# A new issue order for the steady part of a fused short convolution, RMS norm and SwiGLU layer

## The chip, the cores and the metric

The kernel runs on one core of a Trainium2 chip, as one program. The metric is the device time of one execution in microseconds. Shown times are medians of runs on the same chip; the profile is of one further execution, with its own time.

## What is computed

The first stage is a lightweight convolution: softmax weights of 7 taps for each of 8 heads, applied causally along 4096 positions to 8 sequences of 192 channels. The result, 32768 tokens of 192 channels, goes through an RMS norm and a SwiGLU layer of 1536 hidden units, all in float32.

```python
w = softmax(weight, axis=-1)                          # 8 heads x 7 taps
out = np.einsum('hk,bskhg->bshg', w, x_unf)           # causal, 7 taps
x = out.reshape(B * S, D)                             # 32768 x 192
xn = x / sqrt(mean(x * x, -1) + 1e-06) * rms_g
g, val = xn @ w_gate, xn @ w_val                      # 192 x 1536 each
return (g / (1 + exp(-g)) * val) @ w_out              # 1536 x 192
```

## The kernel before, in words

The 32768 tokens are cut into 32 pairs of two tiles of 512 tokens. Pairs 0 and 1 are worked out plainly while the weights are prepared. From pair 2 on, each pair is one block of the steady part: 68 products (gate and value side by side, line 948) and 42 output steps (line 976) on TensorE. Both matrix products are done as 2 x 2 block products with seven instead of eight multiplications, so that sums of blocks stand around them: sums of the input (words x and n, l, d, where n, l and d also split each operand into three parts of fewer bits), sums of products (f1, f3, f4, f5, f6), sums of the hidden values (h1 to h4) and sums of outputs (c1, s7, c2, C22, C21). The hidden units come as six columns of 256, numbered 0 to 5. Columns 0, 2, 4 and 5 take eleven products each, P1 to P7 and Q1 to Q4; columns 1 and 3 take twelve each, A, B and E of the four cells a, b, c and d of the block product.

The order of everything in a block is written out by hand, as words:

- LINE (line 131) is the order of TensorE's 110 words. `P5.2` is product P5 of column 2; `o4.1` is output form 4 with column 1. Before, words 0 to 67 are products, 68 to 109 steps.
- ORDER (line 81) is one round, used for pairs 3 to 31 and once more to finish the last: `p3` issues the next three words of LINE; `Vma.1` issues the word ma.1 on VectorE. The first letter is the engine: V is VectorE, A ScalarE, G GpSimd, S the DMA queue of SyncE. A `+` or `-` at the end means the next or the previous pair, `++` the pair after the next.
- SECOND (line 98) is the round of pair 2, FIRST (line 115) that of pair 1. What FIRST has done ahead for a later pair is not done again in the second round.

`run` (at the end) reads the words. An engine takes its words strictly in this order, and waits for what a word needs from other engines, so a word that has to wait holds up those behind it on its engine. The words that matter here:

- ga to gd are the gates: ScalarE reads a product bank and writes silu into `tt` (line 1031). ma to md multiply by the other half of the bank on VectorE (line 1038) and so make the hidden values. Only when both are done is the bank free; there are four banks, taken and given back by `open` and `give`.
- f1 copies a bank (ScalarE, line 705), f3 copies the first product into c to `tt`. f4 and f5 add on VectorE (line 1025). In column 5 the fifth sum is written to `tt` and f6 adds it to d (line 1018). P7 may add into bank b only after f4 has read it, and Q3 and P4 only after f5.
- h1 to h4 (line 1003) run on VectorE (V) or GpSimd (G); o7 needs h3, o6 needs h2, o3 needs h4 and o5 needs h1. o1 must have read a column before h2 overwrites it, o2 before h4 does.
- C22 and C21 (line 1055) add up the outputs and T11, T12, T21, T22 (line 991) transpose them into `o_sb`, two instructions each; C22 must be done before the o3 steps add into its bank. The stores are the words st, issued by `leave` (line 1087). For the last pair `leave` is called right after the transposes of each half, on ScalarE's and SyncE's queues in turn.
- cv0 to cv6 are the taps of a later pair (line 474; cv0 on ScalarE, line 470), then sq, red, pow, bc and mul (line 524) its norm. pl puts it away to DRAM (line 1098), ft fetches it back as `xb` (line 676), ld loads x (line 174).
- A piece of weights (line 822) is loaded into one of 12 slots, the ring, when the last product that read the slot has been issued. The 48 pieces of a pair are loaded in the order in which LINE first needs them.

Of the kernel before, what the change touches and what calls it, by code (L numbers as in the profile page):

```python
# [20 lines left out]
def kernel(  # L21
# [58 lines left out]
    )  # L80
    ORDER = (
# [15 lines left out]
    )  # L97
    SECOND = (
# [15 lines left out]
    )  # L114
    FIRST = (
# [14 lines left out]
    )  # L130
    LINE = (
# [7 lines left out]
    )  # L139

    cst = ctx.enter_context(tc.tile_pool(name="cst", bufs=1))
# [1213 lines left out]
```

## Time and profile before

| | |
|---|---|
| median of 3 runs | 2448.26 us (2447.83 to 2448.28) |
| the profiled execution | 2448.45 us, its span 2446.6 us |
| mean granted TensorE clock | 0.999 |
| TensorE, VectorE, ScalarE, GpSimd busy | 99%, 88%, 42%, 17% of the span |
| pieces of the longest chain | products (line 948) 57%, output steps (line 976) 36% |
| start of the first block's products | 208.41 us |

A row of the timeline has the start and the length in microseconds, the engine, the line, the operation, output and inputs, the count, and in brackets the idle time of the engine ahead of it with what ended it. PE is TensorE's matmul, PEld its weight load, DVE VectorE, ACT ScalarE, POOL GpSimd; a q behind the name (SPq, ACTq) is the part of an engine that issues DMAs. A row of the groups has the busy time, the mean in nanoseconds of one, and the idle time ahead. In the wait view a row says which engine waited for which, the total in microseconds, how often, and the longest. In the table of stretches each engine has its busy time and its count, then come the clock, the DMA share and GB/s.

### The profile page before, as it was taken

Reading aid. Unit: us, or ns where it says so; the run is one execution under the profiler, and the core shown is the slowest. Engines: PE = TensorE matmul, PEld = TensorE weight load, DVE = VectorE, ACT = ScalarE, POOL = GpSimd, SP = SyncE. Lnnn points to the kernel's source line nnn. Section 1 sums busy time; section 2 is a strip of 40 time slices with the busy share of each in tenths; the row PEclk is TensorE's granted clock in tenths of the full one; section 3 lists DMA queues with packets and bytes.
Section 4 is the critical chain, followed back from the end, with each engine's and each line's share of the span. In section 5 each row is a group of like instructions: output and inputs, shape, how many; then the busy total and the mean of one; then the engine's idle time right before and its main releaser. Section 6 shows DMA issues by size and latency. Waiting matters only on the chain.

```text
span 2446.6 us, 69165 instructions
## 1 busy us (share of the span) xinstructions
PE 2433.7 (99%) x29136; PEld 1947.4 (80%) x29136; DVE 2164.7 (88%) x2822; ACT 1027.1 (42%) x1431; POOL 412.4 (17%) x362
## 2 busy tenths in 40 slices
PE   8999999999999999999999999999999999999999
PEld 5648888888888878878877888777788777878777
DVE  8688988899888899888899888998888998888975
ACT  6443344443344444344443444433444443444432
POOL 0542011110111110111100111101111101111010
PEclk9999999999999999999999999999999999999999
DMA  7375668666677666677666676666776676776653
GB/s 153 61 212 142 171 179 215 188 166 171 175 189 215 174 170 176 177 200 206 160 175 174 181 212 193 164 170 175 190 213 176 169 176 174 203 207 158 174 161 96
DMA packets 716391, 430.54 MB, mean 176 GB/s; under 512 B 510330, under 2 KB 702386, under 8 KB 716082
## 3 DMA queue, kind: packets, MB, share of 16 engines
q1 hardware_dynamic: 712336, 425.21, 66.5%
q8 instruction: 230, 3.77, 0.7%
q10 hardware_dynamic: 3746, 0.92, 0.2%
q14 instruction: 79, 0.65, 0.1%
HBM read 366.96 MB, written 58.98 MB: 174 GB/s over the span
## 4 chain that ended last, share of the span: by engine, by line
PE 96%; DMA 1%; POOL 1%; DVE 1%; SPq 1%; issue 0%; ACT 0%; DVEq 0%; POOLq 0%
PE ps L948 57%; PE ps L976 36%; PE ps L1135 2%; DMA ht<-in_moe_w_val_dram 0%; PE ps L920 0%; POOL ht L1003 0%; SPq L174 0%; POOL part L799 0%; DMA x<-in_x_dram 0%; DMA wd<-part 0%; DVE ht L1003 0%; DMA ht<-in_moe_w_gate_dram 0%; SPq L258 0%; DVE part L795 0%; DVE ht L1038 0%
## 5 line engine op out<-in xcount | busy, mean ns | idle before, releaser
L948 PE MATMUL ps<-part,ring 64*128 64x512 f32 x11304 | 1327.9, 388 | 0.0
L948 PEld LDWEIGHTS ps<-part,ring 64*128 64x128 f32 x11304 | 1117.9, 184 | 176.7 <-DVE tt L1018 11.3
L1031 ACT ACTIVATE tt<-ps 128x512 f32<-128x512 f32 x744 | 438.6, 599 | 718.4 <-PE ps L948 533.6
L1038 DVE TENSOR_TENSOR ht<-ps,tt 128x512 f32<-128x512 f32 x744 | 494.2, 685 | 149.8 <-ACT tt L1031 145.2
L976 PE MATMUL ps<-ht,wo_sb 128*32 128x384 f32 (+2 forms) x7272 | 443.9, 380 | 0.0
L976 PE MATMUL ps<-ht,x 128*32 128x256 f32 (+2 forms) x6696 | 405.2, 379 | 0.3 <-POOL ht L1003 0.3
L976 PEld LDWEIGHTS ps<-ht,wo_sb 128*32 128x32 f32 x7272 | 311.6, 110 | 103.1 <-issue 11.6
L976 PEld LDWEIGHTS ps<-ht,x 128*32 128x32 f32 x6696 | 287.5, 110 | 95.5 <-POOL ht L1003 0.5
L474 DVE SCALAR_TENSOR_TENSOR y<-xh,tp,y 128x1536 f32<-128x1536 f32 x186 | 338.0, 1817 | 1.2
L1025 DVE TENSOR_TENSOR ps<-ps,tt 128x1024 f32<-128x1024 f32 x210 | 258.5, 1231 | 38.9 <-ACT tt L705 28.4
L503 POOL TENSOR_SCALAR r<-r 128x8 f32<-128x8 f32 x31 | 6.1, 198 | 1598.1 <-DVE r L498 1597.9
L705 ACT COPY tt<-ps 128x384 f32<-128x384 f32 (+1 forms) x182 | 151.9, 834 | 258.1 <-PE ps L976 249.4
L1003 DVE TENSOR_TENSOR ht<-ht 128x512 f32<-128x512 f32 x312 | 213.5, 701 | 10.4 <-PE ps L976 9.2
L705 ACT COPY ps<-ps 128x1024 f32<-128x1024 f32 (+1 forms) x151 | 134.0, 887 | 187.5 <-PE ps L976 91.3
L1003 POOL TENSOR_TENSOR hs<-ht 128x512 f32<-128x512 f32 x90 | 115.3, 1296 | 275.1 <-DVE ht L1038 227.8
L705 ACT CAST part<-tt 128x1024 fp32r<-128x1024 f32 x60 | 62.7, 1045 | 187.4 <-DVE tt L868 187.4
L976 PE MATMUL ps<-hs,x 128*32 128x128 f32 (+2 forms) x2232 | 131.6, 379 | 0.0
L976 PEld LDWEIGHTS ps<-hs,x 128*32 128x32 f32 x2232 | 98.2, 110 | 26.9
L1003 DVE TENSOR_TENSOR ht<-hs,ht 128x512 f32<-128x512 f32 x181 | 117.3, 689 | 0.1
L854 DVE TENSOR_TENSOR part<-xb,part 128x1024 fp32r<-128x1024 f32 x87 | 105.9, 1217 | 0.0
L856 DVE SCALAR_TENSOR_TENSOR part<-part,xb 128x1024 fp32r<-128x1024 f32 x87 | 105.8, 1216 | 0.0
L948 PE MATMUL ps<-part,part 64*128 64x512 f32 x720 | 103.9, 387 | 0.0
(137 smaller groups left out, 1573.0 us busy)
## 6 DMA issues: line engine op xcount, KB each, us to landing
ring<-wd SPq DMA_DIRECT2D x1326, 192.0 KB
xb<-xd SPq DMA_DIRECT2D x60, 512.0 KB
xd<-xh SPq DMA_DIRECT2D x240, 96.0 KB
part<-wd SPq DMA_DIRECT2D x114, 192.0 KB
xh<-in_x_dram SPq DMA_DIRECT2D x192, 105.0 KB
xb<-xd SPq DMA_DIRECT2D x60, 256.0 KB
out_dram<-o_sb SPq DMA_DIRECT2D x126, 96.0 KB
out_dram<-o_sb SPq DMA_DIRECT2D x62, 128.0 KB
```

The lines of the kernel that those rows point to most:

```text
L474: nc.vector.scalar_tensor_tensor(out=y, in0=xk, scalar=w, in1=y, op0=ALU.mult, op1=ALU.add)
L503: nc.gpsimd.tensor_scalar(out=r, in0=r, scalar1=s / D, scalar2=s * 1e-6, op0=ALU.mult, op1=ALU.add)
L705: nc.scalar.copy(out=dst, in_=src)
L854: e.tensor_tensor(out=split_of(g, 1).bitcast(F32R), in0=src, in1=high, op=ALU.subtract)
L856: nc.vector.scalar_tensor_tensor(out=split_of(g, 2).bitcast(F32R), in0=high, scalar=1.0 + SPLIT, in1=src, op0=ALU.mult, op1=ALU.subtract,)
L948: nc.tensor.matmul(out=self.both(j, c)[:, h, :], lhsT=left[HALF[h]], rhs=right[HALF[h]], start=(first and q == 0), stop=True, skip_group_c ...
L976: nc.tensor.matmul(out=self.acc(b)[i * Q : (i + 1) * Q, at : at + n], lhsT=left, rhs=cols, start=fresh, stop=True, skip_group_check=True, ...
L1003: engine[eng].tensor_tensor(out=dst, in0=a, in1=b, op=op)
L1025: nc.vector.tensor_tensor(out=self.both(j, c), in0=self.both(j, "b"), in1=s5, op=ALU.add)
L1031: nc.scalar.activation(out=tt[:, t, :], in_=self.both(j, c)[:, 0, :], func=AF.Silu)
L1038: nc.vector.tensor_tensor(out=self.hv(j, "abcd".index(c)), in0=self.both(j, c)[:, 1, :], in1=tt[:, t, :], op=ALU.mult,)
L1135: nc.tensor.matmul(out=bank(h, bks[h])[:], lhsT=wf[HALF[h], AT[h][k], u * NF + f, :], rhs=xb[HALF[h], g, k, :], start=(k == 0), stop=(k == ...
```

## The change

ORDER, SECOND and LINE are written anew, and three words are added at the end of FIRST. No word's work changes, and each block has the same 68 products and 42 steps. What differs:

- LINE has another order. The three products of column 3's cell c (Ac.3, Bc.3, Ec.3), which stood among column 0's products, now stand among column 5's, right ahead of P7.5. P7.5 moves from word 63 to word 62, Q3.5 from 66 to 67, P4.5 from 67 to 66. The output steps follow another order of columns, and so do all words of ORDER around them.
- Four sums go from VectorE to GpSimd: h3.1, h1.2, h3.3 and h2.1. GpSimd has nine of 24 then, not five.
- The last three words of a pair's LINE (o3.0, o3.2, o3.5) are issued at the start of the next round (`p3-`), and T12, T21 and T22 follow there in this order. Before, T22 and T21 stood at the end of the round, and T12 at the start of the next.
- The tap cv4 goes to the round before (`Vcv4++`). For pair 3 it stands at the end of FIRST, with d.4 of pair 2 (and l.2, which FIRST has done already), ahead of C22 of pair 1 on VectorE. In SECOND d.4 stood behind C22 and T11.
- The loads of x (`Sld`) start earlier in the block, at word 61, not 76, and the stores stand elsewhere.

The diff, cut to the rows that the text speaks of:

```diff
     ORDER = (
-        "p1 Vcv5+ p1 VT12- p1 Af1.0 p2 Vcv4+ p2 Aga.1 Vcv6+ p1 Vma.1 p1 Aga.0 p1 Agb.1 Vma.0",
...
-        "Af1.2 Vcv2+ p2 Agc.1 Vmc.1 Af3.2 p2 Sst0.1- p1 Aga.2 p1 Vf4.2 p2 Asq+ p1 Vma.2 Vf5.2",
...
-        "p1 Vf4.5 p2 Vf5.5 Aga.5 Vma.5 p1 Gh1.4 p2 Sft.4+ Vf6.5 Vh3.2 Agd.5 Gh1.3 p1 Agb.5",
-        "Vh3.3 p1 Vh2.0 p5 Vmd.5 Vmb.5 Ac1 Sft.5+ Vh1.5 Agc.5 p1 An.0+ Sst0.4- p1 Vh3.5",
...
-        "Vd.3+ Ac2 Vh4.3 An.2+ Vl.2+ p2 Vh4.0 p1 Vh4.4 p4 Vd.2+ VC22 p2 VT11 p2 Vx3+ VC21",
-        "An.4+ p2 Acv0++ VT22 VT21 p1 Vd.4+ p1",
+        "p3- p1 Vcv5+ Af1.0 p1 VT12- p1 VT21- p1 Vcv1+ VT22- Aga.1 p1 Vma.1 Vl.4 p1 Aga.0 p1",
...
+        "Agd.1 p2 Vmd.1 Agd.0 p2 Agb.0 p1 Vcv6+ Vmb.0 Sst0.3- Vmd.0 p1 Vcv3+ Af1.2 p1 Sst1.0-",
+        "p1 Agc.1 Vmc.1 p1 Sst0.4- Af3.2 Vf4.2 p3 Sst0.0- p1 Aga.2 Sst1.1- p1 Vma.2 Vf5.2 p1",
...
+        "p2 Sft.0+ Af3.5 Sft.2+ p1 Sft.4+ Gh1.2 p2 Vf4.5 Sld.4++ p2 Sft.5+ Aga.5 Vma.5",
+        "Sld.3++ p1 Agc.3 p1 Vf5.5 Gh3.3 Gh1.4 Vh3.2 p1 Sld.7++ Vmc.3 p2 Vf6.5 Agc.5 p2 Agb.5",
+        "Agd.5 Sld.6++ p1 Vmb.5 p1 Vmd.5 Vmc.5 p1 Vh1.5 Sld.5++ p1 Gh3.4 Vh2.0 Sst1.2- p3 Ac1",
+        "p1 Vh2.3 An.0+ Vh3.5 p2 Vh2.2 Gh2.1 p1 Vx3+ Sld.0++ Vh2.4 p2 Vd.0+ An.1+ p1 Vl.1+",
...
+        "Vd.3+ Acv0++ p1 VC22 Vd.4+ Vcv4++ p5 VC21",
     )
     SECOND = (
-        "p2 Vl.2 VC22- VT11- p6- Vd.4 VT22- VT21- Vcv5+ VT12- p1 Af1.0 p4 Aga.1 Sst0.4-",
+        "p2 VC22- VT11- p6- VT22- VT21- Vcv5+ VT12- Af1.0 p2 Aga.1 p1 Vma.1 Vl.4 p1 Aga.0 p1",
...
     FIRST = (
...
-        "VC21 p1 Vh4.4",
+        "VC21 p1 Vh4.4 Vl.2+ Vd.4+ Vcv4++",
     )
     LINE = (
-        "P1.0 Aa.1 Ba.1 Ea.1 Ab.1 P2.0 Q1.0 Eb.1 Bb.1 P5.0 P6.0 Ad.1 Bd.1 Ed.1 Ac.3 P7.0 P3.0",
-        "Q2.0 Ec.3 Bc.3 Q3.0 Q4.0 P4.0 P1.2 Ac.1 Ec.1 Bc.1 P5.2 P6.2 P2.2 Q1.2 Ab.3 P7.2 P3.2",
-        "Q2.2 Bb.3 Q4.2 Q3.2 P4.2 Eb.3 P1.4 Aa.3 Ea.3 Ba.3 P5.4 P6.4 P2.4 Q1.4 Ad.3 P7.4 Q2.4",
-        "P3.4 Ed.3 Bd.3 Q4.4 P1.5 Q3.4 P4.4 P5.5 P6.5 Q1.5 P2.5 Q4.5 P7.5 P3.5 Q2.5 Q3.5 P4.5",
...
+        "P1.0 Aa.1 Ea.1 Ba.1 P2.0 Q1.0 P5.0 P6.0 Ab.1 Eb.1 Bb.1 Ad.1 P3.0 P7.0 Q2.0 Ed.1 Bd.1",
+        "Q3.0 Q4.0 P4.0 P1.2 Ac.1 Bc.1 Ec.1 P5.2 P6.2 Q1.2 P2.2 Ab.3 P7.2 Eb.3 Q2.2 P3.2 Q4.2",
+        "Q3.2 P4.2 Bb.3 P1.4 Aa.3 Ba.3 Ea.3 P5.4 P6.4 Q1.4 P2.4 Ad.3 Bd.3 P7.4 Ed.3 P3.4 Q2.4",
+        "Q4.4 P1.5 P4.4 Q3.4 P5.5 P6.5 Q1.5 P2.5 Ac.3 Bc.3 Ec.3 P7.5 Q4.5 Q2.5 P3.5 P4.5 Q3.5",
```

50 rows, old and new, of tables (LINE, ORDER, SECOND) are left out of this document.

## The prediction

> **What bounds the kernel now.** I read the page first: its span, the busy shares and the chain that ended last.
>
> ```profile
> span 2446.6 us, 69165 instructions
> ...
> PE 2433.7 (99%) x29136; PEld 1947.4 (80%) x29136; DVE 2164.7 (88%) x2822; ACT 1027.1 (42%) x1431; POOL 412.4 (17%) x362
> ...
> PE 96%; DMA 1%; POOL 1%; DVE 1%; SPq 1%; issue 0%; ACT 0%; DVEq 0%; POOLq 0%
> ```
>
> TensorE bounds. Then the table of stretches, for one block (a pair's 68 products and 42 output steps), with the count and busy time of PE, PEld, DVE, ACT and POOL:
>
> ```profile
> 1252.67:1326.96 74.29, 74.29 (x916) 58.64 (x914) 67.34 (x87) 31.23 (x42) 11.39 (x10) 1.00 0.70 183
> ```
>
> A block takes 74.29 us, at full clock, and thirty of them are nearly the whole span. "Busy" can hide a late start, so the block has to be compared with its own undisturbed pace. The next rows, of the timeline, are PE and its weight loads (PEld) at the start and at the end of this block's products, then the last four products of the block two later; last the wait view from 290 to 2400 us (28 blocks):
>
> ```profile
> 1252.67 1.65 PE L948 MATMUL ps<-part,ring 64*128 64x512 f32 x12
> ...
> 1254.62 3.36 PEld L948 LDWEIGHTS ps<-part,ring 64*128 64x128 f32 x30
> ```
>
> ```profile
> 1298.70 0.86 PE L948 MATMUL ps<-part,part 64*128 64x512 f32 x6
> 1299.49 0.52 PE L976 MATMUL ps<-ht,wo_sb 128*32 128x384 f32 x4
> ```
>
> ```profile
> 1444.98 3.16 PE L948 MATMUL ps<-part,ring 64*128 64x512 f32 x24
> 1448.07 1.29 PE L976 MATMUL ps<-ht,wo_sb 128*32 128x384 f32 x18
> ```
>
> ```profile
> PEld ps L948 <- DVE tt L1018: 10.5, 28, 0.4
> PEld ps L976 <- issue: 10.1, 28, 0.4
> PEld ps L948 <- issue: 5.6, 28, 0.2
> ```
>
> Thirty loads are five products (six matmuls each, two at a time): (3.36 - 0.18 for the last load) / 14 = 0.227 us a pair of matmuls, 0.680 a product. 68 products would take 46.25; the part lasts 1299.49 - 1252.67 = 46.82. Of the 0.57 over, 0.13 is the first product's start (1.65 against 5 x 0.227 + 0.386) and 0.11 the change to output steps (the last pair starts at 1298.70 + 0.45, the step 0.34 later, not 0.227): both stay. That leaves 0.33. Most of it is one place: the last four products take 1448.07 - 1444.98 = 3.09 where 2.72 is the pace, 0.37, less the 0.11 of the change: 0.26 us. The wait view names the cause, the only data wait of TensorE in the steady part: the sum of line 1018 (word f5.5), read before Q3.5 may add into the same bank. No row there names a DMA.
>
> **The change part by part.** I number the words of LINE from 0; product k starts near 0.13 + 0.680 k in its block, and steps follow at 27.43 / 42 = 0.653 us.
>
> (1) f5.5 goes earlier against its reader. These are it and f6.5 now:
>
> ```profile
> 1296.62 1.23 DVE L1018 TENSOR_TENSOR tt<-ps,tt 128x1024 f32<-128x1024 f32 x1 [1.12 <-PE ps L948]
> ...
> 1298.36 1.22 DVE L1018 TENSOR_TENSOR ps<-ps,tt 128x1024 f32<-128x1024 f32 x1
> ```
>
> It waits for P7.5 and ends at 1297.85, 45.18 in the block; Q3.5, word 66, was due at 0.13 + 44.88 = 45.01. P7.5 moves from word 63 to 62 while the first reader (P4.5) stays at 66: f5.5 ends 0.68 earlier, at 44.50, 0.5 ahead. So the 0.26 goes. Also P7.4 and P7.5 each stand further behind the products on which their sum f4 waits (six and seven words, five now), which may take some of the other 0.07. At P7.2 the distance is still five words. I take 0.26 a block, 30 x 0.26 = **-7.8 us**; ends: 0 if another wait takes its place, 30 x 0.33 = -9.9.
>
> (2) Four sums of h move from VectorE to GpSimd.
>
> ```profile
> L1003 DVE TENSOR_TENSOR ht<-ht 128x512 f32<-128x512 f32 x312 | 213.5, 701 | 10.4 <-PE ps L976 9.2
> L1003 POOL TENSOR_TENSOR hs<-ht 128x512 f32<-128x512 f32 x90 | 115.3, 1296 | 275.1 <-DVE ht L1038 227.8
> ```
>
> VectorE loses 4 x 0.70 = 2.8 of its 67.3 us a block, GpSimd gains 4 x 1.30 = 5.2 on 11.4; neither is the bound, so I count nothing. What must not get late is C22, on VectorE, which o3.4 (word 104) awaits. Now:
>
> ```profile
> 1301.30 1.28 DVE L1038 TENSOR_TENSOR ht<-ps,tt 128x512 f32<-128x512 f32 x2
> ...
> 1322.18 0.55 DVE L1055 TENSOR_TENSOR tt<-ps,tt 128x384 f32<-128x384 f32 x1
> ```
>
> C22 ends at 1322.73, o3.4 starts at 1299.49 + 36 x 0.653 = 1323.00: 0.27 to spare, and the 42 steps show no stall. Between f6.5 and C22 the new queue has three h less, and x3 and T11 more (0.60 from start to start each: 1.28 - 0.68; T11 0.56): 1.20 - 0.56 = 0.64 less; some 0.4 of it is spent waiting for the gate of word 67, and the steps come 0.26 sooner. The spare time stays near 0.25.
>
> (3) P5.2 goes from word 27 to 24 and opens the bank that md.0 frees; ahead of md.0 stand md.1, the tap cv6 and mb.0. The nearest rows:
>
> ```profile
> 1268.73 1.09 ACT L1031 ACTIVATE tt<-ps 128x512 f32<-128x512 f32 x2 [1.43 <-PE ps L948]
> ...
> 1270.57 1.81 DVE L474 SCALAR_TENSOR_TENSOR y<-xh,tp,y 128x1536 f32<-128x1536 f32 x1
> 1272.30 0.69 DVE L1038 TENSOR_TENSOR ht<-ps,tt 128x512 f32<-128x512 f32 x1
> 1273.14 1.23 DVE L1025 TENSOR_TENSOR ps<-ps,tt 128x1024 f32<-128x1024 f32 x1 [0.15 <-ACT tt L705]
> ```
>
> A gate starts 0.97 after its last product (1268.73 is 16.06; word 22 starts at 15.09). Word 16 ends d.1: gate at 11.01 + 0.97 = 11.98, done 12.58; then 0.60 for md.1, 1.73 for the tap, 0.60 for mb.0, 0.69 for md.0: 16.2. P5.2 is due at 16.45: 0.2 to spare. f4.2 has as much now (ends 21.70, P7.2 due 21.89), and its place has at most the 0.07 of small delays. So I take 0; the upper end is the stall of f5.5, 0.26 a block.
>
> (4) Transfers. Shortest lead of a ring load (from the end of the last product that read its slot to the first that needs it): by LINE eight products now, 5.4 us, then ten, 6.8 us. So the wait view should still name no DMA. SP's queue gets the loads of x earlier, beside the puts:
>
> ```profile
> L822 SPq DMA_DIRECT2D ring<-wd x1326: 315/320/2059, 199.1 to 2403.4; - x190
> L1098 SPq DMA_DIRECT2D xd<-xh x240: 533/617/2278, 140.4 to 2336.5; - x120
> L676 SPq DMA_DIRECT2D xb<-xd x120: 319/414/1382, 105.6 to 2347.6; - x120
> L174 SPq DMA_DIRECT2D xh<-in_x_dram x255: 464/842/3610, 21.6 to 2283.3; - x128
> ```
>
> By the medians (middle figures, ns), words 42 to 67 issue 20 ring loads (6.4), eight puts (4.9), four fetches (1.7), three loads of x (2.5) and two stores of about 0.5: 16.5 us in 17.7. It fits, without room: 0 taken, price under the rivals.
>
> (5) The head, once: d.4 and one tap stood behind the second pair's C22 and T11 (SECOND), and now stand in FIRST, ahead of C22.
>
> ```profile
> 208.53 0.69 DVE L1003 TENSOR_TENSOR ht<-ht 128x512 f32<-128x512 f32 x1 [0.67 <-PE ps L976]
> 209.13 0.55 DVE L1055 TENSOR_TENSOR tt<-ps,tt 128x384 f32<-128x384 f32 x1
> ...
> 209.99 3.84 PEld L976 LDWEIGHTS ps<-ht,wo_sb 128*32 128x32 f32 x72 [0.36 <-DVE tt L1055]
> ...
> 210.16 1.18 DVE L856 SCALAR_TENSOR_TENSOR part<-part,tt 128x1024 fp32r<-128x1024 f32 x1
> ...
> 212.34 1.77 DVE L474 SCALAR_TENSOR_TENSOR y<-xh,tp,y 128x1536 f32<-128x1536 f32 x1
> ```
>
> C22 ends at 209.68 and TensorE goes on at 209.99; all it has meanwhile are two products of the next pair, which it has done by 209.8. With the two operations ahead, C22 and all behind it come 1.18 + 1.77 less some 0.05 of overlap each: **+2.85 us**. Ends: 0 if something hid it (the h sum ahead waits for TensorE, so nothing does), 2.95.
>
> (6) The tail, once: T22 and T21 now follow T12, which waits for the last step.
>
> ```profile
> 2437.94 1.15 DVE L991 STREAM_TRANSPOSE o_sb<-tt 128x256 f32<-128x256 f32 x4
> 2438.92 2.11 ACTq L1087 DMA_DIRECT2D out_dram<-o_sb  x3
> ...
> 2441.36 0.65 DVE L991 STREAM_TRANSPOSE o_sb<-ps 128x256 f32<-128x256 f32 x2 [2.28 <-PE ps L976]
> 2441.84 2.16 ACTq L1087 DMA_DIRECT2D out_dram<-o_sb  x3
> ```
>
> The 1.15 us of transposes and the first half's stores fall behind the end of TensorE. ScalarE's queue then issues six stores in a row, its last three 2.1 us later than now: **+2.1 us**; ends 1.15 (the transposes alone) and 3.
>
> Sum, against the profiled execution's 2448.45 us (span 2446.6 and 1.85 around it): -7.8 + 2.85 + 2.1 = -2.85, **2445.6**. The median of the runs, 2448.26, lies 0.2 lower: I say **2445.4 us**, -0.12%. A measurement of this kernel can tell about 0.2%, 4.9 us, from no change.
>
> [...] Early on GpSimd and VectorE slow each other, both with two operands in SBUF (first the usual time of the VectorE operation, then the timeline):
>
> ```profile
> L854 DVE TENSOR_TENSOR part<-xb,part 128x1024 fp32r<-128x1024 f32 x87 | 105.9, 1217 | 0.0
> ```
>
> ```profile
> 185.34 9.88 POOL L1003 TENSOR_TENSOR ht<-hs,ht 128x512 f32<-128x512 f32 x5 [7.54 <-PE ps L976]
> ...
> 188.37 2.30 DVE L854 TENSOR_TENSOR part<-ring,part 128x1024 fp32r<-128x1024 f32 x1
> ...
> 1295.19 1.29 POOL L1003 TENSOR_TENSOR hs<-ht 128x512 f32<-128x512 f32 x1
> ```
>
> There a GpSimd sum takes 1.98 (9.88 / 5), not 1.29, and VectorE's 1.22 becomes 2.30. In the steady part GpSimd's sums run beside gates read from PSUM, at full speed (1295.19 beside f5.5). [...]
>
> **The rivals.**
> (A) As summed: 2445.4.
> (B) Faster: all 0.33 a block goes and the tail costs only the transposes: -9.9 + 2.85 + 1.15 = -5.9, **2442.4**. For it: the longer distances of P7.4 and P7.5. Against: P7.2 keeps its five.
> [...]
> (D) Another bank wait takes the place of the old one, at P5.2 or P7.2, at the old price: 30 x 0.26 = 7.8 back, **2453**, at the edge of what can be told. The 0.2 to spare speaks against it, its thinness for it.
> (E) SP's queue: it blocks on the first put until the scaling on GpSimd is done, runs over its 17.7 us, and ring loads come late; 0.5 us a block would be +15, **2460**. Against: the lead grows by 1.4 us.
> (F) The change isn't what its words say: in LINE all three products of column 3 (Ac.3, Bc.3, Ec.3) stand ahead of P7.5, none behind. The sums above use LINE as it stands, so this changes no number.
>
> **How the numbers follow.** A 0.38 (0.03 of it below the 0.2% line), B 0.25 (0.01 above it), D 0.14 (half past the line on the slow side), C 0.13, E 0.10. Faster 0.27 (0.03 + 0.24), within 0.2% 0.43 (0.35 + 0.01 + 0.07), slower 0.30 (0.07 + 0.13 + 0.10). The range runs from 2440.5 (B with the tail near nothing) to 2456, which holds A, B, D and a C of lighter price, and leaves out E and the rest: 0.2. A's own is 2443 to 2448.
>
> **What would show it.** Right: the wait of PEld for line 1018 gone or tiny; blocks of 74.0 us; the first steps after C22 near 212.8 instead of 209.99; after the last step, transposes of 1.8 us and six stores in a row. Wrong: a new row of PE or PEld behind line 1038 (D), 1055 or 1025, steps slower than 0.653 (C), or a row that names a DMA (E); GpSimd's sums above 1.3 us.

## The result, and the profile after

| | before | after the change |
|---|---|---|
| median of 20 runs each | 2448.27 us (2447.72 to 2450.64) | 2453.15 us (2447.44 to 2460.67) |
| the profiled execution | 2448.45 us, span 2446.6 | 2452.15 us, span 2450.4 |
| start of the first block's products | 208.41 us | 208.49 us |
| block of pair 2, of pair 3 | 78.53, 74.29 us | 84.52, 76.11 us |
| blocks of pairs 4 to 30, mean | 74.29 us | 74.06 us (21 of the 27 take 73.92 to 74.03) |
| from the start of the last block to the end | 79.7 us | 81.6 us |

The ratio is 1.0017 (95% interval 1.0010 to 1.0024): slower by 0.17%, where 0.12% faster was forecast. The runs of the changed kernel also spread over 13 us, those of before over 3.

The page's first rows, and then the table of stretches for the blocks of pairs 2, 3 and 9 (columns as in the prediction):

```profile
span 2450.4 us, 69381 instructions
...
PE 2429.1 (99%) x29136; PEld 1979.6 (81%) x29136; DVE 2090.1 (85%) x2702; ACT 1033.3 (42%) x1431; POOL 565.3 (23%) x482
```

```profile
208.49:293.01 84.52, 78.35 (x986) 65.17 (x984) 66.40 (x87) 31.50 (x42) 16.48 (x14) 1.00 0.65 161
293.01:369.12 76.11, 76.00 (x912) 67.15 (x912) 65.44 (x83) 31.52 (x42) 16.48 (x14) 0.98 0.76 179
735.30:809.30 74.00, 74.00 (x918) 63.94 (x914) 64.80 (x83) 31.41 (x43) 16.48 (x14) 1.00 0.76 184
```

The ordinary block is 0.3 us shorter, as forecast. Pair 2's block lasts 84.52 us with PE busy for 78.35 only, and pair 3's has a granted clock of 0.98. The wait view of PEld, 290 to 2400 us:

```profile
PEld ps L976 <- issue: 11.8, 32, 0.7
PEld ps L948 <- issue: 5.9, 29, 0.4
PEld ps L948 <- DVE tt L1055: 4.1, 2, 3.9
PEld ps L948 <- DVE ps L1025: 1.3, 4, 0.4
PEld ps L948 <- DVE ht L1038: 0.3, 1, 0.3
```

The old row (line 1018, 28 times) is gone. In its place stands one long wait, 3.9 us behind line 1055, C21. The timeline of the end of pair 2's block tells what C21 waited for:

```profile
289.06 1.57 ACT L470 ACTIVATE y<-xh,tp 128x1536 f32<-128x1536 f32 x1 [4.73 <-DMA xh<-in_x_dram]
290.67 1.82 DVE L474 SCALAR_TENSOR_TENSOR y<-xh,tp,y 128x1536 f32<-128x1536 f32 x1 [4.69 <-ACT y L470]
292.41 0.55 DVE L1055 TENSOR_TENSOR tt<-ps,tt 128x384 f32<-128x384 f32 x1
...
293.01 9.36 PE L948 MATMUL ps<-part,ring 64*128 64x512 f32 x65 [3.64 <-DVE tt L1055]
```

Read it upwards. P1.0 of pair 3 waits for the bank that C21 frees; C21 itself waited for nothing on TensorE, but stands behind the tap cv4 in VectorE's queue; cv4 needs cv0 on ScalarE; cv0 needs the last load of x, which landed 4.73 us late. So a load that no product of this block reads stops TensorE, through two engines' queues. The two waits exist in the wait views of ScalarE and VectorE (290 to 2400 us) only after the change:

```profile
ACT y L470 <- DMA xh<-in_x_dram: 8.3, 7, 4.7
```

```profile
DVE y L474 <- ACT y L470: 7.5, 7, 4.7
```

Two things had moved towards each other. cv0 is due sooner: in the block of pair 9 it starts 72.2 us after the block's first product before the change (block from 732.6) and 68.9 us after it now (from 739.2). First the row of before, then that of after:

```profile
804.81 1.58 ACT L470 ACTIVATE y<-xh,tp 128x1536 f32<-128x1536 f32 x1
```

```profile
808.14 1.58 ACT L470 ACTIVATE y<-xh,tp 128x1536 f32<-128x1536 f32 x1
```

And cv4 used to stand in the next round, where nothing urgent was behind it; now C21 is. By the DMA records of its packets, the last load lands 66 to 71 us into an ordinary block before the change and 66 to 69 us after it: at least 1.4 us of slack before, hardly any now.

The pause costs twice. Granted clock (third number from the right) around it:

```profile
289.00:293.00 4.00, 0.37 (x8) 0.10 (x2) 2.33 (x3) 1.57 (x1) 0.00 (x0) 1.00 0.00 0
293.00:297.00 4.00, 3.99 (x21) 3.19 (x23) 4.00 (x6) 1.00 (x1) 0.00 (x0) 0.57 0.18 49
297.00:301.00 4.00, 4.00 (x38) 3.44 (x36) 3.66 (x7) 2.21 (x3) 0.00 (x0) 1.00 0.22 57
```

After 3.64 us without work, TensorE gets 21 matmuls done in 4 us where 38 is the pace: 0.43 x 4 = 1.7 us more, which is most of what pair 3's block lost. (The 0.57 is a mean over 4 us: the trace has the clock at 0.50 for 3.41 us, from 293.28 to 296.69.)

Why were pair 2's loads so late? SyncE's queue in that stretch:

```profile
264.42 2.24 SPq L1087 DMA_DIRECT2D out_dram<-o_sb  x1
266.80 4.07 SPq L822 DMA_DIRECT2D ring<-wd  x2
270.92 0.52 SPq L676 DMA_DIRECT2D xb<-xd  x1
271.49 0.93 SPq L174 DMA_DIRECT2D xh<-in_x_dram  x1
272.52 1.00 SPq L822 DMA_DIRECT2D ring<-wd  x1
273.57 2.44 SPq L1087 DMA_DIRECT2D out_dram<-o_sb  x3
...
281.77 3.16 SPq L174 DMA_DIRECT2D xh<-in_x_dram  x4
```

SECOND puts four of pair 1's stores among pair 2's loads: 4.7 us of stores in these rows alone, with a ring load at 2 us instead of the usual 0.3, ahead of the last loads.

A third loss is small and scattered. In pairs 3, 16 and 22 the steps themselves stand still, 0.5 to 0.8 us each, with no releaser in the trace:

```profile
1315.28 0.79 PEld L976 LDWEIGHTS ps<-ht,wo_sb 128*32 128x32 f32 x15 [0.72 <-issue]
```

Before, no step did. TensorE's program arrives in packets of 16 KB (3.77 MB in 230): from 290 us on one lands for every 253 of the trace's TensorE instructions, as 2 x 29136 over 230 packets gives too. The row has their count, MB and share of the engines' time:

```profile
q8 instruction: 230, 3.77, 0.7%
```

If each packet's landing is counted in TensorE's own instructions, against the mean course, the five latest packets, some 150 to 170 instructions behind, are those of pairs 16, 22, 30, 23 and 3: from pair 3 on, the five blocks whose steps take more than 27.44 us. The latest packet of before is some 105 behind. And between 48 and 56 us of a block the DMA share is 1.10 to 1.14 (mean of 26 blocks), where it was 0.98 to 1.03. (The share is the time of the packets begun in a stretch against that of 16 engines, so it can exceed 1.) So after the change the blocks with the latest packets are those that stall, which fits steps that wait for their program but doesn't prove it.

The head and the tail came as forecast. Head:

```profile
209.22 1.22 DVE L856 SCALAR_TENSOR_TENSOR part<-part,tt 128x1024 fp32r<-128x1024 f32 x1
...
210.36 1.81 DVE L474 SCALAR_TENSOR_TENSOR y<-xh,tp,y 128x1536 f32<-128x1536 f32 x1
212.09 0.55 DVE L1055 TENSOR_TENSOR tt<-ps,tt 128x384 f32<-128x384 f32 x1
...
212.69 2.40 PEld L976 LDWEIGHTS ps<-ht,wo_sb 128*32 128x32 f32 x48 [2.97 <-DVE tt L1055]
```

The steps resume at 212.69, not 209.99: 2.70 us, against 2.85 summed. Here PE paused for 2.5 us, and its clock stayed at 1.00, which was not so in every run (last section). Tail:

```profile
2442.86 0.65 DVE L991 STREAM_TRANSPOSE o_sb<-ps 128x256 f32<-128x256 f32 x2 [3.34 <-PE ps L976]
2443.34 4.28 ACTq L1087 DMA_DIRECT2D out_dram<-o_sb  x6
2443.43 1.11 DVE L991 STREAM_TRANSPOSE o_sb<-tt 128x256 f32<-128x256 f32 x4
```

Transposes of 1.7 us and six stores in a row behind the last step; the last block and its tail take 81.60 us where they took 79.67: 1.93 us more.

### The profile page after: what moved, and what is told of

Its sections match the earlier page's. It is cut to its first block, busy times and chain, and to the rows that moved or that the text cites. A ratio compares the mean times of both kernels' runs of the same rounds, so it can differ in the third digit from the quotient of the medians.

```text
span 2450.4 us, 69381 instructions
## 1 busy us (share of the span) xinstructions
PE 2429.1 (99%) x29136; PEld 1979.6 (81%) x29136; DVE 2090.1 (85%) x2702; ACT 1033.3 (42%) x1431; POOL 565.3 (23%) x482
## 3 DMA queue, kind: packets, MB, share of 16 engines
q8 instruction: 230, 3.77, 0.7%
## 4 chain that ended last, share of the span: by engine, by line
PE 95%; DMA 1%; DVE 1%; POOL 1%; SPq 1%; issue 0%; ACT 0%; DVEq 0%; ACTq 0%; POOLq 0%
PE ps L948 57%; PE ps L976 35%; PE ps L1135 2%; SPq L174 0%; PE ps L920 0%; DMA ht<-in_moe_w_val_dram 0%; POOL ht L1003 0%; POOL part L799 0%; DVE ht L1003 0%; DMA x<-in_x_dram 0%; DMA wd<-part 0%; DMA xh<-in_x_dram 0%; SPq L258 0%; DMA ht<-in_moe_w_gate_dram 0%; DVE y L474 0%
## 5 line engine op out<-in xcount | busy, mean ns | idle before, releaser
L948 PE MATMUL ps<-part,ring 64*128 64x512 f32 x11160 | 1307.8, 387 | 3.6 <-DVE tt L1055 3.6
L976 PE MATMUL ps<-ht,wo_sb 128*32 128x384 f32 (+2 forms) x7272 | 429.4, 380 | 2.6 <-DVE tt L1055 2.5
L976 PE MATMUL ps<-ht,x 128*32 128x256 f32 (+2 forms) x6696 | 411.0, 379 | 0.4 <-POOL ht L1003 0.3
L976 PEld LDWEIGHTS ps<-ht,wo_sb 128*32 128x32 f32 x7272 | 319.0, 110 | 99.4 <-issue 12.5
L1003 POOL TENSOR_TENSOR hs<-ht 128x512 f32<-128x512 f32 x120 | 155.2, 1294 | 169.1 <-DVE ht L1038 127.8
L705 ACT COPY tt<-ps 128x384 f32<-128x384 f32 (+1 forms) x182 | 151.6, 833 | 86.9 <-PE ps L976 76.8
L1003 DVE TENSOR_TENSOR ht<-ht 128x512 f32<-128x512 f32 x252 | 169.7, 705 | 4.7 <-PE ps L976 4.6
L1003 POOL TENSOR_TENSOR ht<-ht 128x512 f32<-128x512 f32 x120 | 154.0, 1294 | 2.3
L976 PE MATMUL ps<-hs,x 128*32 128x128 f32 (+2 forms) x2232 | 143.9, 379 | 0.0
L948 PE MATMUL ps<-part,part 64*128 64x512 f32 x912 | 129.8, 386 | 0.0
L976 PEld LDWEIGHTS ps<-hs,x 128*32 128x32 f32 x2232 | 103.7, 110 | 25.5
```

Source lines behind the costliest of these rows:

```text
L705: nc.scalar.copy(out=dst, in_=src)
L948: nc.tensor.matmul(out=self.both(j, c)[:, h, :], lhsT=left[HALF[h]], rhs=right[HALF[h]], start=(first and q == 0), stop=True, skip_group_c ...
L976: nc.tensor.matmul(out=self.acc(b)[i * Q : (i + 1) * Q, at : at + n], lhsT=left, rhs=cols, start=fresh, stop=True, skip_group_check=True, ...
L1003: engine[eng].tensor_tensor(out=dst, in0=a, in1=b, op=op)
```

## The experiments

Theory T1: the loss is the chain above. Rivals: R1, the new order is too tight on VectorE and the banks whatever the loads do; R2, ring loads come late. T2, for the scattered rest, came later. Each group of runs has the kernel before beside it on the same chip; differences below are against that median, whose own value moved from 2447.4 to 2449.2 between groups.

### Moving the loads, or C21

In the first two, loads 0, 2 and 1 of x stand 9 to 13 words earlier (`loads_early` in both rounds, `second_only` in SECOND alone); in `loads_late` they stand later. An excerpt of `loads_early`:

```diff
-        "p1 Vh2.3 An.0+ Vh3.5 p2 Vh2.2 Gh2.1 p1 Vx3+ Sld.0++ Vh2.4 p2 Vd.0+ An.1+ p1 Vl.1+",
+        "p1 Sld.1++ Vh2.3 An.0+ Vh3.5 p2 Vh2.2 Gh2.1 p1 Vx3+ Vh2.4 p2 Vd.0+ An.1+ p1 Vl.1+",
...
-        "Vh4.4 Sld.1++ p1 Vh4.1 Vd.2+ p1 Vh4.5 Vl.2+ Vl.3+ Ac2 p2 Vd.1+ p3 Vx4+ p2 An.4+ p1",
+        "Vh4.4 p1 Vh4.1 Vd.2+ p1 Vh4.5 Vl.2+ Vl.3+ Ac2 p2 Vd.1+ p3 Vx4+ p2 An.4+ p1",
```

> The new order with the last three loads of x (0, 2, 1) issued 9 to 13 words earlier, in ORDER and SECOND. Theory T1 (loads of x land after the tap cv0 is due; cv4 waits for cv0, C21 stands behind cv4, and the next block's P1.0 waits for the bank that C21 frees): the waits of ScalarE at line 470 for DMA and of VectorE at line 474 for ScalarE vanish; pair 2's block falls from 84.5 to about 81 us, pair 3's from 76.1 to about 74.1, and blocks 15 and 30 lose their 0.3 to 0.5; the time is 2445 to 2447 us and the spread of the runs shrinks to about 3 us. Rival R1 (the new order is simply too tight on VectorE and the banks, whatever the loads do): unchanged, 2453 us. Rival R2 (SyncE's queue is full, so that moving loads only moves the lateness to the ring): a ring load comes late, TensorE waits for DMA, over 2453 us.

> The same edit in SECOND alone, the round of pair 2. T1: pairs 2 and 3 recover their 3.6 and 2 us, the scattered losses of later blocks (some 2 us) stay: 2447 to 2448.5 us. R1: unchanged, 2453 us.

> The opposite dose: the last three loads of x 6 to 7 words (some 4 us) later in ORDER. T1: in each of 28 blocks the last load lands near 72 to 74 us, cv0 (due at 68.9) waits 3 to 5 us, P1.0 waits 2.5 to 4.5 us and TensorE starts the block at a lower clock: 80 to 160 us more, 2530 to 2610 us. R1: within 5 us of 2453.

Measured: +1.9 us (2450.59; 2446.99 to 2452.74), +1.8 us (2450.51; 2447.33 to 2458.30), and 2446.88 in the one run of `loads_late`. All three missed, and not as R1 or R2 say: pair 2's block still took 84.4 and 86.9 us in the first two, with the same chain (1.7 of the 86.9 is a slow clock in the head, see the last section). The edits did not do what they say. Between words 68 and 98 SyncE has nothing but these loads and one store, and a word that moves past another engine's words moves past nothing in its own queue. `loads_late` is thus the same program as the changed kernel, one run more, in which the loads happened to land 1 us late, not 4.7 (pair 2's block 80.8 us). `second_only` only changes the order of the loads among themselves, and `loads_early` puts two of them ahead of one store besides. So the cause stayed untested, but one thing follows: the same program has the loss or hasn't, by how late the loads land. Three profiles of this one program (the changed kernel, `after_again` below, `loads_late`) have cv0 of pair 2's block waiting 4.73, 1.82 and 0.98 us, and that block at 84.52, 81.62 and 80.80 us.

`c21_first` changes VectorE's own queue:

```diff
-        "Vd.3+ Acv0++ p1 VC22 Vd.4+ Vcv4++ p5 VC21",
+        "Vd.3+ Acv0++ p1 VC22 Vd.4+ p5 VC21 Vcv4++",
```

> The loads stay late, but C21 stands ahead of the tap cv4 on VectorE. T1: P1.0 no longer waits behind the late tap (the row of 3.6 us is gone), and TensorE's clock is not lost after it; the late tap then holds up T12, the taps and the gates of the next block, so 1 to 3 us come back there in pair 3: 2448 to 2451 us. R1: unchanged, 2453 us.

Measured: +1.9 us (2450.62; 2446.04 to 2456.26; ratio 1.0004, 0.9995 to 1.0013). The load is as late as ever (cv0 waits 5.0 us), but pair 2's block takes 80.81 us and no wait of 3.6 us stands at its end. Pair 3's takes 78.16 instead; PE's timeline there:

```profile
288.65 4.37 PE L948 MATMUL ps<-part,ring 64*128 64x512 f32 x36
294.59 1.67 PE L948 MATMUL ps<-part,ring 64*128 64x512 f32 x12 [1.57 <-DVE o_sb L991]
297.93 3.84 PE L948 MATMUL ps<-part,ring 64*128 64x512 f32 x30 [1.67 <-DVE ht L1038]
```

The late tap now holds up T12 and the next block's gates, in two shorter pauses and at full clock. That is T1's chain with another victim, as expected, and it speaks against R1: the same order without the late tap ahead of C21 has no stall at P1.0. The median says nothing here, as `loads_early` and `second_only`, which kept the chain, came out at +1.9 and +1.8 beside it. R2 has no row: in the changed kernel's blocks, here and in its other profiles, nothing of TensorE waits for a DMA.

### What stands ahead of the loads in SyncE's queue

`second_stores` takes pair 1's stores in SECOND from words 46 to 66 to words 8 to 20. `after_again` is the changed kernel, run beside it.

```diff
-        "Af3.0 Vma.0 p4 Vf4.0 p1 Agb.1 p1 Sst0.4- p1 Sst0.2- p1 Sst1.4- Vmb.1 p2 Vf5.0 Agc.0",
+        "Af3.0 Vma.0 p4 Vf4.0 p1 Agb.1 p1 Sst0.4- Sst0.3- p1 Sst0.2- Sst0.0- p1 Sst1.4- Sst0.1- Vmb.1 p2 Vf5.0 Agc.0 Sst1.0- Sst1.1-",
...
-        "Agc.3 p1 Vf5.5 Sst1.0- Gh3.3 Sst1.2- Gh1.4 Sst1.3- Vh3.2 p1 Sld.7++ Vmc.3 p2 Vf6.5",
+        "Agc.3 p1 Vf5.5 Gh3.3 Gh1.4 Vh3.2 p1 Sld.7++ Vmc.3 p2 Vf6.5",
```

> The changed kernel once more, as the reference of this call: 2450 to 2454 us, runs spread over 5 us or more, depending on how late the loads of x land in the round of pair 2 (2446.9 to 2460.7 so far).

> The changed kernel with pair 1's stores in SECOND taken ahead (words 8 to 20), ORDER as it is. T1: pair 2's block near 80.9 us and pair 3's near 74.0 in the profile, no wait of P1.0 there; the high runs go; 2 to 5 us below after_again. If pair 2's late loads are a minor part: within 1 us.

Measured: `after_again` +4.3 us (2453.54; 2449.00 to 2456.60; ratio 1.0016, 1.0007 to 1.0025), `second_stores` +0.3 us (2449.53; 2447.95 to 2453.27; ratio 1.0002, 0.9993 to 1.0011). Pairs 2 and 3 take 80.94 and 73.93 us. SyncE's last rows there, and the stretch in which the clock had dropped:

```profile
270.97 1.91 SPq L174 DMA_DIRECT2D xh<-in_x_dram  x2
272.92 1.88 SPq L178 DMA_DIRECT2D xh<-x  x1
274.85 3.17 SPq L174 DMA_DIRECT2D xh<-in_x_dram  x4
```

```profile
293.00:297.00 4.00, 4.00 (x38) 3.32 (x36) 4.00 (x5) 1.78 (x3) 0.00 (x0) 1.00 0.61 174
```

The last four loads are issued 7 us sooner, and 38 matmuls run where 21 did. The 4.0 us between the two medians is T1's, shown by taking away what stood ahead of the load (the profiled run of `after_again`, 2449.47, lies 4 us below its median, with pair 2's block at 81.62). Some 3 us are left against the forecast. In the profile of `second_stores`, steps stand still for 2.1 us, and TensorE waits 4.0 us for banks (lines 1055, 1025, 1038), with loads of x still late in seven later blocks (5.6 us in all).

Four kernels of an earlier group add up edits on this base: `stores` (in ORDER too, the one store among the loads behind them), `stores_head` (the head's two operations back behind C22), `stores_head_tail` (T21 and T22 ahead of T12 in the last round alone), and on top of that `reader_near`:

```diff
-        "Vh4.4 Sld.1++ p1 Vh4.1 Vd.2+ p1 Vh4.5 Vl.2+ Vl.3+ Ac2 p2 Vd.1+ p3 Vx4+ p2 An.4+ p1",
+        "Vh4.4 Sld.1++ Sst1.2- p1 Vh4.1 Vd.2+ p1 Vh4.5 Vl.2+ Vl.3+ Ac2 p2 Vd.1+ p3 Vx4+ p2 An.4+ p1",
...
-        "VC21 p1 Vh4.4 Vl.2+ Vd.4+ Vcv4++",
+        "VC21 p1 Vh4.4",
...
+        if w == PAIRS:
+            at = words.index("VT12-")
+            words.remove("VT21-")
+            words.remove("VT22-")
+            words[at:at] = ["VT21-", "VT22-"]
...
-        "Q4.4 P1.5 P4.4 Q3.4 P5.5 P6.5 Q1.5 P2.5 Ac.3 Bc.3 Ec.3 P7.5 Q4.5 Q2.5 P3.5 P4.5 Q3.5",
+        "Q4.4 P1.5 P4.4 Q3.4 P5.5 P6.5 Q1.5 P2.5 Ac.3 Bc.3 Ec.3 P7.5 Q4.5 Q2.5 P4.5 P3.5 Q3.5",
```

> The new order, with pair 1's stores in SECOND taken ahead of the loads of x (from words 46 to 66 to words 8 to 20), and in ORDER the one store that stands among the loads (Sst1.2-) behind the last load. T1, mended by what loads_early and loads_late showed (SyncE's queue runs late, so that what counts is how much stands ahead of a load in the queue, not its word): the last load of pair 2's round lands 5 to 7 us earlier, near 74 us; P1.0's wait of 3.7 us there and the slow clock after it go, pairs 2 and 3 fall from 84.5 and 76.1 us to near 81 and 74.2; the later waits of cv0 lose about half: 2445.5 to 2447.5 us, runs within 4 us. R1 (the order itself is too tight): unchanged, 2453 us.

> As stores, and d.4 of pair 2 and the tap cv4 of pair 3 taken from the end of FIRST to SECOND, behind C22 and T11. The steps after C22 resume near 210.0, not 212.7: 2.7 us below stores, 2443 to 2445 us, unless the tap delays a gate of pair 2 (then up to 1 us of it comes back).

> As stores_head, and in the last round alone T21 and T22 stand ahead of T12, so that the first half is transposed and stored while TensorE does the last steps: 2 us below stores_head, 2441 to 2443 us, 0.2% to 0.3% faster than the kernel before.

> As stores_head_tail, with P4.5 and P3.5 exchanged in LINE, so that the first reader of f5.5's sum stands three words behind P7.5 again, as before the change, not four. If the steady gain came from that distance, PEld waits for line 1018 again, 0.2 to 0.3 us in each of 29 blocks, and the time is 6 to 9 us above stores_head_tail. If the gain came from elsewhere (the order of the columns, the earlier distances): within 2 us of it.

Measured, against 2449.13: +0.3 (2449.45), -5.1 (2444.03), -7.5 (2441.67) and +0.7 us (2449.79). `stores` missed by 2 us: its profile has the good pair 2 (80.90 us), but six blocks with steps that stand still, 2.9 us in all. The head gave 5.4 us, twice its term, where pair 2's block differs by 2.7 in the profiles; where the rest comes from is not shown (the runs of the two spread over 6.7 and 5.5 us). The tail gave 2.4. And `reader_near` is 8.1 us slower than its base, with the old row back:

```profile
PEld ps L948 <- DVE tt L1018: 10.7, 28, 0.4
PEld ps L976 <- DVE ps L1018: 6.2, 17, 0.4
```

(The second row is no new wait. It is the regular start of the steps, 10 us by "issue" elsewhere, put down to another releaser in 17 blocks.) Nothing moved but the first reader of f5.5's sum, from four words behind P7.5 to three. So the steady gain, 8.1 / 30 = 0.27 us a block, is that distance.

### The four sums on GpSimd

`h_vector` puts h3.1, h1.2, h3.3 and h2.1 back on VectorE, on `stores_head_tail`:

```diff
-        "p1 Vh2.3 An.0+ Vh3.5 p2 Vh2.2 Gh2.1 p1 Vx3+ Sld.0++ Vh2.4 p2 Vd.0+ An.1+ p1 Vl.1+",
+        "p1 Vh2.3 An.0+ Vh3.5 p2 Vh2.2 Vh2.1 p1 Vx3+ Sld.0++ Vh2.4 p2 Vd.0+ An.1+ p1 Vl.1+",
```

> As stores_head_tail, with the four sums h3.1, h1.2, h3.3 and h2.1 back on VectorE. Term (2) of the prediction: VectorE gets 4 x 0.70 us more a block; of these h2.1 alone stands between f6.5 and C22, whose spare time is near 0.25 us, so C22 ends about 0.45 us late and o3.4 waits 0.2 to 0.5 us in each of 28 blocks: 6 to 14 us more, 2448 to 2456 us. If the order has room on VectorE: within 2 us of stores_head_tail.

Measured: +6.4 us (2453.78), 13.9 above its base by the two differences. The steps of every block take 27.89 us or more, not 27.44, and the wait view has a new row for o3.4:

```profile
PEld ps L976 <- DVE tt L1055: 13.1, 25, 0.8
```

So the 0.25 us that C22 had to spare were real: 0.70 us more ahead of it makes 0.45 a block. On GpSimd, at 1.29 us each, the sums leave the steps at 27.44, and the order needs them there.

### The scattered stalls

T2: SyncE's transfers, bunched in the new order, delay TensorE's instruction packets. `loads_68` puts all loads of x behind word 76, as before the change; `before_early` gives the kernel before the new order's early loads; `fetch_late` takes `loads_68` and puts the last two fetches where they were before the change. One line of each:

```diff
-        "Vl.0+ p1 Sld.2++ Vx1+ Vh2.5 Vx2+ p2 An.3+ As7 Vh4.2 Vh4.0 Vh4.3 p2 VT11 p1 An.2+ p1",
+        "Vl.0+ Sld.5++ p1 Vx1+ Sld.0++ Vh2.5 Vx2+ p2 An.3+ As7 Sld.2++ Vh4.2 Vh4.0 Vh4.3 p2 VT11 p1 An.2+ p1",
```

```diff
-        "p1 Vf4.5 p2 Vf5.5 Aga.5 Vma.5 p1 Gh1.4 p2 Sft.4+ Vf6.5 Vh3.2 Agd.5 Gh1.3 p1 Agb.5",
+        "p1 Vf4.5 Sld.1++ p2 Vf5.5 Aga.5 Vma.5 Sld.0++ p1 Gh1.4 p2 Sft.4+ Sld.7++ Vf6.5 Vh3.2 Agd.5 Gh1.3 p1 Agb.5",
```

```diff
-        "p2 Sft.0+ Af3.5 Sft.2+ p1 Sft.4+ Gh1.2 p2 Vf4.5 p2 Sft.5+ Aga.5 Vma.5",
+        "p2 Sft.0+ Af3.5 Sft.2+ p1 Gh1.2 p2 Vf4.5 p2 Aga.5 Vma.5",
...
+        "p1 Agc.3 p1 Vf5.5 Sft.4+ Gh3.3 Gh1.4 Vh3.2 p1 Vmc.3 p2 Vf6.5 Agc.5 p2 Agb.5",
+        "Agd.5 p1 Vmb.5 p1 Vmd.5 Vmc.5 p1 Vh1.5 p1 Gh3.4 Vh2.0 p3 Ac1 Sft.5+",
```

> As stores_head_tail, with all loads of x behind word 76, where the kernel before has them, and so behind every ring load of the block in SyncE's queue. Theory T2 (the second part of the loss: the first loads of x, now beside the ring loads, over-fill the DMA engines, 1.10 to 1.14 of full between 48 and 56 us of the block where the kernel before has 0.98 to 1.03, and TensorE's 16 KB instruction fetches land so late that output steps stand still in some blocks, the rows 'PEld L976 <- issue' beyond the regular 0.35): DMA share there falls to 1.05 or less, the scattered stalls of the steps go, the runs spread over less than 3 us. The loads land at 66 to 69 us, cv0 is due at 68.9: a few short waits. 2439 to 2441 us. Rival R3 (the scattered stalls have nothing to do with the loads of x): the stalls stay, 2441 to 2443 us or more if cv0 waits longer.

> The converse: the kernel before, with its loads of x at the words that the new order gives them (61 to 91) and nothing else. T2: DMA share between 48 and 56 us rises to about 1.1, steps show stalls by issue in 2 to 7 of 28 blocks, the time rises 1 to 3 us and the runs spread over 4 us or more; cv0, due at 72, still doesn't wait. R3: within 0.5 us of the kernel before.

> As loads_68, with the last two of the four fetches of xb (ft.4, ft.5: 512 or 256 KB each) back behind words 63 and 76, where the kernel before has them; the new order has all four between words 58 and 62. T2, mended by loads_68 (the loads of x alone do not fill the DMA engines: their share is still 1.05 to 1.08 between 48 and 56 us of the block, and three blocks still stand still in their steps): the fetches are the other part; the share falls to 1.0, the 16 KB instruction fetches land in time and the scattered stalls of the steps (2.9 us in all in loads_68's profile) shrink below 1 us: 2437 to 2439 us against a kernel before of 2448. If the ring loads alone fill the engines, or the stalls come from something else: within 1 us of loads_68. Against it: x is split from xb, so a fetch too late would show as a wait of ScalarE at line 705 for DMA.

Measured: `loads_68` -7.3 us (2440.11; 2439.03 to 2445.27), no better than its base at -7.5, with 2.9 us of stalls left in three blocks: the loads of x alone are not all of it. That profile is of its slowest run, though; six of the eight runs take 2439.0 to 2440.5. `before_early` +1.9 us (2449.33; ratio 1.0006, 0.9997 to 1.0015), not told from no change; its DMA share did not rise as meant (1.00 and 0.85), and a fetch came late instead (ScalarE waits for xb, 7.4 us in 9 waits), so it doesn't decide. `fetch_late` -9.2 us (2439.11; 2438.81 to 2439.93), ratio 0.9964 (0.9950 to 0.9977): the fastest kernel here. Its wait view of PEld, whole:

```profile
PEld ps L976 <- issue: 9.9, 28, 0.4
PEld ps L948 <- issue: 5.6, 28, 0.2
```

Only the regular start of steps and products is left; every block from pair 3 to 30 takes 73.94 to 73.98 us. The share of the DMA engines hardly fell (1.04 and 1.11), against the expectation; the latest packet is some 150 instructions behind, without a stall. So SyncE's order as a whole removes the stalls: all but one, of 0.55 us, where `queue_only`, below, changes nothing else. That the last two fetches are needed for it is not shown, since the intervals of `loads_68` (0.9962 to 0.9982) and `fetch_late` overlap. That late packets are the cause fits the traces, and which quantity of the DMA engines decides stays open.

`fetch_only` makes the same move of the fetches on the changed kernel, whose loads of x then stand ahead of them; `stores_fetch` adds the stores of `second_stores`.

> The changed kernel with the last two fetches of xb (ft.4, ft.5) back behind words 63 and 76, in ORDER and SECOND; all else as it is, the loads of x too. T2 mended: the scattered stalls by issue between steps go (1.5 to 3 us), while the loads of x, now beside two fetches, land no earlier, so cv0's waits stay or grow: 0 to 3 us below after_again. If the stalls had gone in fetch_late because of the loads and the fetches together: no change.

> Both edits. If the two causes add up, 4 to 7 us below after_again, 2445 to 2447 us, which is the forecast of the prediction (2445.4) with head and tail still paid; spread below 3 us.

Measured: +86.6 (2535.79) and +82.8 us (2531.95), far off. ScalarE's and PEld's wait views of `fetch_only`:

```profile
ACT part L705 <- DMA xb<-xd: 113.5, 27, 5.7
```

```profile
PEld ps L976 <- ACT tt L705: 47.9, 26, 3.3
PEld ps L976 <- DVE tt L1055: 27.2, 21, 1.3
```

Behind five loads of x in SyncE's queue, the last fetch lands 4.2 us late on average, in 27 of 28 blocks; ScalarE's cast waits for it, the output sums on ScalarE stand behind the cast, and the steps wait for them. It is the same kind of chain as pair 2's, in every block.

`queue_only` puts SyncE's queue alone in order (stores of SECOND early, fetches as in `fetch_late`, loads of x behind all of them) and leaves the change's head and tail.

> The changed kernel with SyncE's queue alone put in order, as in fetch_late: pair 1's stores early in SECOND, the loads of x behind word 76 and behind all four fetches, ft.4 and ft.5 behind words 63 and 76; head and tail as the change has them. If the queue is all that the forecast missed, every block from pair 3 on takes 73.95 us, and the time is fetch_late's 2439.1 with 2.7 of the head and 2.0 of the tail on top: 2443 to 2445 us, 0.15 to 0.2% below the kernel before, with runs within 2 us. If something else was missed: 2447 us or more.

Measured: -4.6 us (2444.14; 2443.43 to 2445.96), ratio 0.9982 (0.9973 to 0.9991). Pair 2's block takes 81.09 us, and 26 of the next 28 take 73.92 to 74.01; its runs spread over 2.5 us, not 13. Every word but SyncE's stands where the change has it, so R1 falls with it.

## Why the prediction was wrong, step by step

It said 2445.4; the median is 2453.15. In the profiled executions the change cost 3.7 us (2452.15 against 2448.45) where the sum said -2.85: 6.55 us apart. Of these pair 2's block and its start have 3.5, pair 3's 2.1, pairs 4 to 30 together 0.9, the end 0.1.

- **Step (4), transfers, failed.** It put "0 taken" on a queue that "fits, without room", and rival (E) gave the queue a price only through *ring loads*. No ring load came late. The loads of x did, and step (4) never asked when they must have landed: cv0 moved 3.3 us towards them, and cv4 moved to a place where C21 stands behind it. The step counted the length of SyncE's issues by their medians; by the DMA records, a load of the new order lands some 2 to 8 us after its issue. It also looked at the steady block alone, where SECOND, with four stores among the loads of pair 2, was worst. Priced by the runs, the step is worth 4.0 us for SECOND's stores (`second_stores`), and the whole queue turns +4.3 to +4.9 into -4.6 (`queue_only`).
- **Step (1) was right**, and low: 0.26 a block summed, 0.32 in 21 blocks, 0.27 of it by `reader_near` alone. The sums f4 with their longer distance may have the rest, as (B) held; this was not tried by itself.
- **Step (2) was right**: no stall at o3.4, GpSimd's sums at 1.29 us. The 0.13 for C, a block made slower by sums of GpSimd and VectorE that meet, rests on a price that no run shows: between 290 and 2400 us of the changed kernel's profile no sum on GpSimd overlaps an h sum or a split on VectorE, and h2.1 ends 0.30 us before h1.5 starts. `h_vector` bears out the spare time. One reading was off: the sum at 1295.19 ends 0.14 us before f5.5 starts; the one beside f5.5 is the next, from 1296.44, and takes 1.30 us all the same.
- **Step (3) was right** in ordinary blocks. Banks are waited for (lines 1025 and 1038, 1.6 us in five waits) mostly in a block behind a late tap.
- **Steps (5) and (6) were right** in these profiles: 2.70 for 2.85, 1.93 for 2.1. But (5) has no term for the clock, which fell after the head's pause in three of the eleven profiles that have it, at 1.7 us each.
- **(F) was right** and changed no number.
- **That the time lies in the stated range, and at D's 2453, is luck.** D has a bank wait of 0.26 in each of 30 blocks; banks cost 1.6 us in five waits.

With the queue in order, the forecast's own terms give the forecast: `queue_only` is 4.6 us below before, -2.85 by the sum and 0.06 x 30 = 1.8 more by the larger steady gain.

## What to carry to other kernels

For each word that an edit moves *earlier*, follow its inputs back to the DMA that brings them, and compare its due time with when the transfer lands, not when it is issued (2 to 8 us earlier here); then ask what stands behind the word on its engine. In `loads_late` words moved past other engines' words alone, and the program stayed the same. A queue is only changed by what moves past words of the *same* queue, so before a transfer is moved, list that queue alone, the odd rounds at the ends too. Where a change makes runs spread out (13 us here, 3 before), look for a wait with no slack rather than for a longer operation.

## What was not expected of the hardware

- **A pause of 2.0 to 3.4 us cost TensorE its clock or not, by when it fell.** In the head of the changed kernel a pause of 2.53 us left the clock at 1.00; in `second_only` the same pause, of 2.54 us, halved it for 3.41 us:

```profile
209.15:212.56 3.41, 0.87 (x14) 0.40 (x14) 3.41 (x6) 0.00 (x0) 0.00 (x0) 1.00 0.20 58
212.56:215.97 3.41, 3.41 (x40) 2.53 (x34) 2.74 (x6) 1.00 (x1) 0.00 (x0) 0.50 0.02 5
```

In each of the 19 traces all changes of the granted clock lie on a grid of 3.41 us. The clock fell at the end of every step of that grid in which TensorE had stood idle for 2.04 us or more, and after no step with 1.95 or less. So a pause of 3.39 us that two steps share (1.84 and 1.55 us, `stores_fetch`) kept the clock, and one of 2.04 us within a step (`fetch_only`) lost it. The pauses of 3.48, 3.64 and 4.27 us at the start of pair 3 (`loads_early`, the changed kernel, `second_only`) all lost it. So 2.04 idle of 3.41 us were enough here; between 1.95 and 2.04 these traces show nothing.
- **Two fetches moved 6 and 14 words later in one queue cost 82 us** where loads of x then stand ahead of them (`fetch_only` against `after_again`, `stores_fetch` against `second_stores`), and nothing where the loads stand behind (`fetch_late` against `loads_68`, 1.9 us less, which the intervals don't tell from none).
